# A list scheduler's model of transfers: issue time and one shared pipe, a margin at landing, and new places

## The chip, the cores and the metric

The kernel runs on one core of one Trainium2 chip. The metric is the device time of one launch in microseconds (us). The core has five instruction streams that run beside each other and wait for one another by semaphores: TensorE (PE in the profile, with its weight loads as PEld), VectorE (DVE), ScalarE (ACT), GpSimd (POOL) and SyncE (SP), which here issues all the transfers. Each engine works off its own stream strictly in the order in which the program was written.

## The reference

```
scores = q @ k.T / sqrt(64) - log(448)
attn   = sigmoid(scores);   x = attn @ v            # 8 batches, 12 heads, 448 x 64
x      = heads side by side                         # (8, 448, 768)
u      = x + (x.T @ U @ V).T                        # U 448 x 32, V 32 x 448
out    = u + relu(u @ w_ch1) @ w_ch2                # 768 -> 3072 -> 768
```

All inputs and the output are float32.

## The kernel before

Large float32 products are made of three float16 products: an operand is scaled by a power of two and split into a high part and a rest, and high x high, high x rest and rest x high are accumulated in one bank of PSUM. The eight banks, the weights (two buffers for each of w1 and w2), the loads of q, k and v (three and four buffers), and the results of attention (UA for batch 0, UB for the others) are all shared by what runs beside each other.

The work falls into these stages:

- Attention of batches 0 and 1 in float32 (the `whole` way, below `WHOLE` = 2): scores (L515), sigmoids on ACT (L631), products with v (L534, L544), then `mix` for U and V.
- The head: the feed-forward part (FFN) of batch 0 in six groups `g`, while the weights are decoded for the first time (`decode`, L836). They arrive as 64-bit words in 48 pieces of 768 KB: a load, three DVE instructions that make float32 of them (`to_f32`), a `bound` on ACT (L436, an absolute sum for the scale), a scale, the high part on ACT or POOL, the rest on DVE (L382). A decoded weight is written to `scratch` in DRAM for the later batches.
- The middle: the FFN of batches 1 to 3 (`ffn_in` L894, `ffn_out` L914) with weights fetched from `scratch`, and beside it the attention of batches 2, 4, 3, 5, 6 and 7 in the split way. There each pair of heads is prepared first: a `bound` of q, k and v, its maximum over the partitions by two transfers (`scale_by_dma`, L408), high parts on POOL, rests on DVE. `mix_half` transposes by a transfer (L803) ahead of its products (L811). `quarter_sums` and `far_forms` prepare sums of weights and of inputs for the last stage.
- The last stage (from about 985 us): the FFN of batches 4 to 7 in two pairs, as products of 2 x 2 blocks with seven instead of eight multiplications (L1089), on forms prepared in DRAM.

The order of all instructions is made by a planner (`Plan`). Every step is entered with `op`: engine, a cost, its operands, a place `pos`, a slack and a landing time. Places are not times, though they are written in the same unit: `order` (L127) simulates all engines, takes the engine and step that can start first, and among those of an engine that can start at that moment the step with the lowest place. What comes out is only the order on each engine and the buffers chosen, and `emit` writes the instructions in that order. A wrong cost therefore doesn't change what is computed; it changes which step stands ahead of which on an engine, where the one behind must wait.

The constants at L60 to L68 set the places. `START` and `ROOM0`, `ROOM` lay the FFN of the four plain batches out: `BEGIN[0]` = `START`, `BEGIN[1]` = `BEGIN[0]` + 163.6 + `ROOM0`, and so on. `BEFORE`, `PACE` and `MIXED1` place the attention of batch 1 and its mixing, `AHEAD`, `PREP` and `BOUNDS` those of the later ones. `DECODE` is how far ahead of a group's place its decode is placed, `EV_IN` and `EV_OUT` by how much the evictions of `ffn_in` and `ffn_out` are placed ahead of their products. `LEAD`, `SUMS`, `STEP_K` and `STEP_I` place the loads and sums of the last stage. A transfer was planned by `load` (L358) as

```
op("SP", max(0.6, n / 0.30e6), ..., land=2.0)
```

so SP is held until its `n` bytes have moved at 0.30 MB per us, and the data is there 2.0 us later. Other transfers had their own costs: the transpose 1.0 and 7.0, the copies to `forms` 0.6 and 3.0. In both versions SP may not start a transfer before the eighth last one has landed.

Of the kernel before, what the change touches and what calls it, by code (L numbers as in the profile page):

```python
# [37 lines left out]
P = 128  # L38
D = 64
# [50 lines left out]
class Plan:  # L90
# [36 lines left out]
    def order(self):  # L127
# [17 lines left out]
        done, port, landed, mode = [], 0.0, [0.0] * 8, 128  # L145
# [21 lines left out]
        while len(done) < n:  # L167
# [58 lines left out]
def fused_kernel(ctx: ExitStack, tc: tile.TileContext, q, k, v, wu, wv, w1, w2, out):  # L226
# [131 lines left out]
    def load(dst, src, n, reads, writes, pos, land=2.0):  # L358
        op("SP", max(0.6, n / 0.30e6), lambda: nc.sync.dma_start(out=dst(), in_=src()), reads, writes, pos, land=land)
# [14 lines left out]
    def pe(cost, fn, reads, writes, pos, slack=0.8, after=(), modes=(128, 128)):  # L374
        return op("PE", cost, fn, reads, writes, pos, slack, 0.3, after, modes=modes)
# [32 lines left out]
    def scale_by_dma(parts, kp, n, name, pos):  # L408
# [3 lines left out]
        load(lambda: far.x, lambda: parts.x[:, :n], 0.18e6, kp, [far], pos, 4.5)  # L412
        load(lambda: row.x[:, : n * P], lambda: far.x.rearrange("p n -> (p n)").partition_broadcast(P), 0.2e6, [far], [row], pos, 5.0)
        m, x = (lambda: e.x[:, :n]), (lambda: e.x[:, n : 2 * n])
        dve(0.15 + n * 0.13, lambda: nc.vector.tensor_reduce(
            out=m(), in_=row.x[:, : n * P].rearrange("q (p n) -> q n p", n=n), axis=AX.X, op=ALU.max), [row], [e], pos)
        dve(0.17, lambda: ts(nc.vector, x().bitcast(I32), m().bitcast(I32), 0x7F800000, ALU.bitwise_and), [e], [e], pos)
        pool(0.35, lambda: ts(nc.gpsimd, inv.x, x(), 2.0 ** -100, ALU.max, 1.0 / TOP, ALU.mult), [e], [inv], pos)
# [56 lines left out]
    def shifted(at):  # L475
        pool(0.5, lambda: nc.gpsimd.memset(ux, 0.0), (), ["ux", "vraw"], at)
        dve(0.25, lambda: nc.vector.tensor_copy(ux[0:64, 0], ua[0:64, 3]), [("ua", i) for i in range(4)] + ["ux"], ["ux"], at)
        load(lambda: ux[64:128, :, 3], lambda: ua[0:64, :, 0], 0.18e6, [("ua", 0), "ux"], ["ux"], at, 4.5)
        load(lambda: ux[0:64, 1:4, 3], lambda: ua[64:128, 0:3, 0], 0.18e6, [("ua", 0), "ux"], ["ux"], at, 4.5)
# [71 lines left out]
    def pair(b, p, at, d):  # L551
# [20 lines left out]
        else:  # L572
# [5 lines left out]
            for i in range(2):  # L578
                bound(lambda i=i: qk.x[:, i, :], S, lambda i=i: ss.x[:, i : i + 1], kqk[2 * i : 2 * i + 2], (ss, i), prep - BOUNDS, 0.73)
            bound(lambda: v32.x.rearrange("p a b -> p (a b)"), 512, lambda: ss.x[:, 2:3], [(v32, 0), (v32, 1)], (ss, 2), prep - BOUNDS, 0.82)  # L580
            s, inv = scale_by_dma(ss, [(ss, i) for i in range(3)], 3, "qkv", prep - BOUNDS + 1)
            cc, cv = sm("c", 1), sm("cv", 1)
            pool(0.5, lambda: ts(nc.gpsimd, cc.x, inv.x[:, 0:1], inv.x[:, 1:2], ALU.mult, 1.0 / math.sqrt(D), ALU.mult), [inv], [cc], prep + 1)
            pool(0.45, lambda: ts(nc.gpsimd, cv.x, inv.x[:, 2:3], 1.0 / A_UP, ALU.mult, 1.0, ALU.mult), [inv], [cv], prep + 1)
            pool(0.45, lambda: ts(nc.gpsimd, cm.x[mine], cc.x[mine], 1.0, ALU.mult, 1.0, ALU.mult), [cc], [(cm, odd)], prep + 1)
# [12 lines left out]
            for i in (1, 0):  # L598
# [3 lines left out]
                dve2(0.63, lambda i=i: rest(part(2 * i + 1), qk.x[:, i, :], s.x[:, i : i + 1], part(2 * i)),  # L602
                    ki + [s, (st, 2 * i)], [(st, 2 * i + 1)], prep + 3)
            pool(0.65, lambda: scaled(parts_v(0), v32.x[:, :3], s.x[:, 2:3]), [(v32, 0), s], [(sv, 0)], prep + 6, plan.wrote["decoded"])
            dve2(0.58, lambda: rest(parts_v(1), v32.x[:, :3], s.x[:, 2:3], parts_v(0)), [(v32, 0), s, (sv, 0)], [(sv, 1)], prep + 7)
            pool(0.45, lambda: scaled(last_v(0)[mine], v32.x[mine, 3], s.x[mine, 2:3]), [(v32, 1), s], [(v3, odd, 0)], prep + 7, plan.wrote["decoded"])
            dve2(0.25, lambda: rest(last_v(1)[mine], v32.x[mine, 3], s.x[mine, 2:3], last_v(0)[mine]), [(v32, 1), s, (v3, odd, 0)], [(v3, odd, 1)], prep + 8)
# [70 lines left out]
    def fetch_u(b, side, pos):  # L678

        u32s[b] = [plan.tile(f"u{side}{c}", [(UA if side == "a" else UB)[c]]) for c in range(NP)]  # L680
        for c in range(NP):
            load(lambda c=c: u32s[b][c].x, lambda c=c: parked[b][:, c], P * S * 4, [("parked", b, c)], [u32s[b][c]], pos + 3.0 * c, 2.5)
# [87 lines left out]
    def u_parts(b, at):  # L770
# [5 lines left out]
        for c in range(NP):  # L776
            hi, lo = (us, c, 0), (us, c, 1)
            if c % 2:
                pool(0.75, lambda c=c: scaled(us.x[:, c, 0, :], u32[c].x, su.x), [ku[c], su], [hi], at)
            else:  # L780
                act(0.65, lambda c=c: nc.scalar.activation(us.x[:, c, 0, :], u32[c].x, AF.Copy, scale=su.x), [ku[c], su], [hi], at)
            dve2(0.63, lambda c=c: rest(us.x[:, c, 1, :], u32[c].x, su.x, us.x[:, c, 0, :]), [ku[c], su, hi], [lo], at)
# [6 lines left out]
    def mix_half(b, hf, pos):  # L789
# [6 lines left out]
        for c in cs:  # L796
            i = c % 3
            if i == 1:
                pool(0.75, lambda c=c, i=i: scaled(xs.x[:, i, 0], u32[c].x, sx.x), [u32[c], sx], [(xs, i, 0)], pos)
            else:  # L800
                act(0.65, lambda c=c, i=i: nc.scalar.activation(xs.x[:, i, 0], u32[c].x, AF.Copy, scale=sx.x), [u32[c], sx], [(xs, i, 0)], pos)
            dve2(0.63, lambda c=c, i=i: rest(xs.x[:, i, 1], u32[c].x, sx.x, xs.x[:, i, 0]), [u32[c], sx, (xs, i, 0)], [(xs, i, 1)], pos)
        op("SP", 1.0, lambda: nc.sync.dma_start_transpose(out=xt.x, in_=xs.x.rearrange("p c x s -> p (c x s)")),  # L803
           [(xs, i, x) for i in range(3) for x in range(2)], [xt], pos + 1.0, land=7.0)
# [31 lines left out]
    def decode(i, g, pos):  # L836
# [5 lines left out]
        for n in range(NPIECE):  # L842
# [4 lines left out]
            bound(lambda t=t: t.x, PIECE, lambda n=n: ss.x[:, n : n + 1], [t], (ss, n), pos + n, 1.03, w64)  # L847
# [5 lines left out]
        for n, t in enumerate(made):  # L853
# [3 lines left out]
            if g == 0 and (i == 0 or n % 2):  # L857
                pool(1.5, lambda t=t, cut=cut: scaled(w.x[:, 0, cut], t.x, s.x), [t, s], [hi], at)
# [77 lines left out]
    def quarter_sums(i, g, f, pos, b=None, after=(), copy_after=()):  # L936
# [17 lines left out]
        for n_, r, c in ((A11, 0, 0), (A12, 0, 1), (A22, 1, 1)):  # L954
            for x in range(2):
                op("SP", 0.6, lambda n_=n_, r=r, c=c, x=x: nc.sync.dma_start(out=far(n_, x), in_=cut(far_w, r, c, x)),
                   [("scratch", i, g)], [("forms", i, n, n_, x)], pos, land=3.0, after=copy_after)
                done.append(("forms", i, n, n_, x))
        four_ = ((1, 0), (1, 1), (0, 0), (0, 1))
        if b is None:  # L960
            w = plan.tile("wsrc", WSRC)
            for j, (r, c) in enumerate(four_):
                for x in range(2):
                    op("SP", 0.7, lambda j=j, r=r, c=c, x=x: nc.sync.dma_start(out=w.x[:, x, j], in_=cut(far_w, r, c, x)),
                       [("scratch", i, g)], [(w, j, x)], pos - 8, land=2.5, after=after)
# [6 lines left out]
        for j in range(4):  # L972
            pool(1.0, lambda j=j: nc.gpsimd.tensor_tensor(out=t.x[:, j], in0=quarter(j, 0), in1=quarter(j, 1), op=ALU.add),  # L973
# [7 lines left out]
        dve2(1.9, lambda: nc.vector.tensor_tensor(out=o.x[:, :, :, 1], in0=t.x.rearrange(order), in1=o.x[:, :, :, 0], op=ALU.subtract),  # L981
             [(t, j) for j in range(4)] + [(o, 0)], [(o, 1)], pos)
        load(lambda: far(slice(S3, S4 + 1), slice(0, 2)), lambda: o.x, P * 24 * P * 2, [(o, 0), (o, 1)], [("forms", i, n, S3)], pos + 1, 3.0)
# [25 lines left out]
    def far_forms(b0, b1, su, pos, step):  # L1009
# [7 lines left out]
        def get(c, r, n):  # L1017
            t, b, part = place(), (b0, b1)[n], c + 3 * r
            op("SP", 0.8, lambda: nc.sync.dma_start(out=t.x, in_=parked[b][:, part]), [("parked", b, part)], [t], at[0], land=2.5)
# [330 lines left out]
```

## Time and profile before

| | us |
|---|---|
| median of 3 runs | 1586.39 (1579.51 to 1586.65) |
| the profiled execution | 1570.29 |
| its span, first to last instruction | 1568.5 |
| ACT busy in it | 815.4 |
| POOL busy in it | 398.7 |

A profile is one execution. Busy time of an engine is the union of its instructions; PE's instructions are pipelined. In the views below, a row of a timeline has the start, the duration, the engine, the line and the operation, output <- inputs, shapes and count, and in brackets the idle time of the engine before it with what ended it. Releasers are inferred from semaphores: the last one to come is named, not what held it up in its turn.

### The profile page before, as it was taken

The page shows a single profiled execution, that of the slowest core. Times are in us where ns is not written, and L with a number is a line of the kernel's source. Part 1 is how long each engine was busy: PE and PEld are TensorE (multiplying, and loading weights), DVE is VectorE, ACT ScalarE, POOL GpSimd, SP SyncE. Part 2 cuts the span into 40 slices and gives each one's busy share as a digit, 9 for nine tenths or more (in the row PEclk, how much of TensorE's full clock was granted, in tenths as well). Part 3 has the DMA queues.
Part 4 walks back from the last instruction along what each step waited for, and adds up shares of the span by engine and source line. Part 5 has one row for each costly group of instructions (what it writes and reads, how often), then busy time and mean ns, then how long its engine had stood idle before and what let it go on. Part 6 is the DMA issues. An engine that isn't in the chain of part 4 may idle for free.

```text
span 1568.5 us, 24119 instructions
## 1 busy us (share of the span) xinstructions
PE 1529.3 (98%) x8843; PEld 753.5 (48%) x8843; DVE 1134.4 (72%) x1904; ACT 815.4 (52%) x1455; POOL 398.7 (25%) x537
## 2 busy tenths in 40 slices
PE   8989989999999999999999999999999999999999
PEld 3345444444444444444444444555555555555554
DVE  2889989777677777777787846776767878564656
ACT  6667655278657567766877653332423614121310
POOL 0100002553323553223212362064454400000000
PEclk9999999999999999999999999999999999999999
DMA  6878887877776877756778547886656673333331
GB/s 216 275 274 291 286 275 245 286 263 187 152 226 153 241 248 201 203 169 172 212 226 232 137 153 246 288 266 196 199 176 195 253 265 123 106 111 136 106 106 71
DMA packets 212567, 320.19 MB, mean 204 GB/s; under 512 B 130016, under 2 KB 178528, under 8 KB 200160
## 3 DMA queue, kind: packets, MB, share of 16 engines
q1 hardware_dynamic: 212448, 318.65, 65.5%
q8 instruction: 69, 1.13, 0.3%
q14 instruction: 50, 0.41, 0.1%
HBM read 247.04 MB, written 77.42 MB: 207 GB/s over the span
## 4 chain that ended last, share of the span: by engine, by line
PE 84%; DVE 7%; DMA 5%; ACT 2%; issue 1%; SPq 0%; POOL 0%; ACTq 0%; DVEq 0%; POOLq 0%
PE bank L1089 36%; PE bank L894 18%; PE bank L914 15%; PE bank L534 5%; PE bank L515 5%; DVE stg L382 1%; DMA qk__99<-k_in 1%; PE bank L544 1%; PE bank L519 1%; DVE a L382 1%; DMA qk__100<-k_in 1%; PE bank L811 1%; ACT at L631 1%; DMA w<-w_in 1%; DVE w__89 L382 0%
## 5 line engine op out<-in xcount | busy, mean ns | idle before, releaser
L382 DVE SCALAR_TENSOR_TENSOR a<-at,a 128x896 f16<-128x896 f32 x126 | 142.0, 1146 | 32.0 <-ACT a L661 31.5
L914 PE MATMUL bank<-h__92,w__90 128*128 128x448 f16 x792 | 158.3, 353 | 0.0
L914 PE MATMUL bank<-h__93,w__91 128*128 128x448 f16 x792 | 157.9, 353 | 0.0
L894 PE MATMUL bank<-us__86,w__88 128*128 128x448 f16 x648 | 130.8, 359 | 7.4 <-DVE ua__74 L382 4.4
L894 PE MATMUL bank<-us__86,w__89 128*128 128x448 f16 x648 | 129.8, 356 | 3.9 <-DVE ua__74 L382 2.7
L894 PEld LDWEIGHTS <-w__88 128*128 128x128 f16 x864 | 84.8, 99 | 92.1 <-issue 17.1
L894 PEld LDWEIGHTS <-w__89 128*128 128x128 f16 x864 | 83.5, 98 | 87.7 <-issue 13.1
L914 PEld LDWEIGHTS <-w__90 128*128 128x128 f16 x864 | 82.4, 98 | 83.1 <-issue 9.8
L914 PEld LDWEIGHTS <-w__91 128*128 128x128 f16 x864 | 82.7, 98 | 82.4 <-issue 9.0
L661 ACT ACTIVATE a<-at 128x896 f16<-128x896 f32 x126 | 116.1, 959 | 0.8
L1089 PEld LDWEIGHTS <-w__89 128*128 128x128 f16 x819 | 80.1, 98 | 74.8 <-issue 0.4
L1089 PEld LDWEIGHTS <-w__88 128*128 128x128 f16 x756 | 74.0, 98 | 69.0
L1089 PEld LDWEIGHTS <-w__91 128*128 128x128 f16 x756 | 74.0, 98 | 68.9
L977 POOL TENSOR_TENSOR w<-w 128x384 f32<-128x384 f32 x96 | 104.4, 1087 | 4.7
L1089 PEld LDWEIGHTS <-w__90 128*128 128x128 f16 x693 | 67.8, 98 | 64.1 <-issue 0.9
L515 PE MATMUL bank<-stg 64*128 64x448 f16 x648 | 75.1, 351 | 3.0 <-ACT at L631 1.9
L973 POOL TENSOR_TENSOR w<-w 128x384 f32<-128x384 f16 x48 | 45.9, 980 | 125.6 <-DVE xnt L981 82.2
L534 PE MATMUL bank<-a,stg 128*64 128x448 f16 x648 | 69.6, 360 | 0.4 <-DVE a L382 0.4
L379 POOL TENSOR_SCALAR inv_qkv__211<-e_qkv__208 128x3 f32<-128x3 f32 x12 | 3.8, 314 | 210.8 <-DVE e_qkv__208 L379 210.7
L631 ACT ACTIVATE at<-bank,bias_s,c__219 128x448 f32<-128x448 f32 x72 | 47.6, 722 | 12.0 <-PE bank L515 5.6
L980 ACT CAST xnt<-w 128x1536 f16<-128x1536 f32 x24 | 35.3, 1471 | 34.6 <-POOL w L977 33.1
L901 ACT ACTIVATE r__94<-bank 128x448 f32<-128x448 f32 x48 | 25.9, 539 | 50.1 <-PE bank L894 50.0
(1132 smaller groups left out, 3150.6 us busy)
## 6 DMA issues: line engine op xcount, KB each, us to landing
w<-w_in SPq DMA_DIRECT2D x48, 768.0 KB, 5.6
forms<-xnt SPq DMA_DIRECT2D x24, 768.0 KB, 4.6
w__89<-forms SPq DMA_DIRECT2D x13, 1344.0 KB, 5.9
w__88<-forms SPq DMA_DIRECT2D x12, 1344.0 KB, 5.7
w__91<-forms SPq DMA_DIRECT2D x12, 1344.0 KB, 5.9
w__90<-forms SPq DMA_DIRECT2D x11, 1344.0 KB, 5.8
forms<-scratch SPq DMA_DIRECT2D x144, 96.0 KB, 3.9
w__88<-scratch SPq DMA_DIRECT2D x9, 1536.0 KB, 8.2
```

The source lines that it names most:

```text
L382: nc.vector.scalar_tensor_tensor(out=out, in0=in0, scalar=s, in1=in1, op0=op0, op1=op1)
L515: nc.tensor.matmul(sc[j, h].x[:, :S], x[rows_of(h), j * P : j * P + P], y[rows_of(h)], start=i == 0, stop=i == n - 1)
L534: nc.tensor.matmul(av.x[rows_of(h), :S], x[:, j, rows_of(h)], y(tiles[j], h), start=j == 0 and i == 0, stop=not quad and j == 2 and i == n ...
L631: act(cost, lambda: nc.scalar.activation(out_(), in_(), AF.Sigmoid, bias=bias_s, scale=c if whole else by.x), kin + ["bias"] + ([] if whol ...
L661: act(0.95, lambda a=a, to=to: nc.scalar.activation(half(a, 0), to.x, AF.Copy, scale=A_UP), kto, [(a, 0)], here + A_OFF)
L894: nc.tensor.matmul(ph.x[:, :S], wx[:, x, c, f * P : (f + 1) * P], us.x[:, c, y, :], start=c == 0 and i == 0, stop=c == NP - 1 and i == 2,)
L901: act(0.54, lambda: nc.scalar.activation(r.x, ph.x[:, :S], AF.Relu, scale=DOWN_H), [ph], [r], pos - EV_IN)
L914: nc.tensor.matmul(po.x[:, :S], wx[:, x, f, e * P : (e + 1) * P], h.x[:, f, y, :], start=f == 0 and i == 0, stop=f == FC - 1 and i == 2,)
L973: pool(1.0, lambda j=j: nc.gpsimd.tensor_tensor(out=t.x[:, j], in0=quarter(j, 0), in1=quarter(j, 1), op=ALU.add), [(w, j, 0), (w, j, 1)] i ...
L977: pool(1.0, lambda o_=o_, x=x, y=y, sub=sub: nc.gpsimd.tensor_tensor(out=t.x[:, o_], in0=t.x[:, x], in1=t.x[:, y], op=ALU.subtract if sub ...
L980: act(1.45, lambda: nc.scalar.copy(o.x[:, :, :, 0], t.x.rearrange(order)), [(t, j) for j in range(4)], [(o, 0)], pos)
L1089: nc.tensor.matmul(bank.x[:, :S], wt.x[:, k, FACTOR[n], x], both(f)[:, y], start=start and k == i == 0, stop=k == 2 and i == 2, skip_group ...
```

## The change

Three things in the planner, and nothing in the instructions.

A transfer holds SP only for its issue (0.42 to 0.7 us, 3.9 for the transpose). Its bytes then go through one pipe at 0.33 MB per us, shared by all transfers, and the data is there 3.7 us after they are through (some have 0.3 to 1.5 more). The end so told also frees the buffers. Some costs of ACT, DVE and POOL steps are corrected by some hundredths to 0.5 us. `LATE` keeps the slack of PE's steps at the 0.8 that it had. All places are set anew.

```diff
-ROOM0, ROOM, AHEAD, BEFORE, PACE = 43.592, 38.551, 48.926, 33.326, 1.302
-PREP, BOUNDS, VALUES, SECOND, MIXED = 13.847, 6.504, 1.154, 1.456, 5.983
+PIPE, LANDS, LATE = 0.33e6, 3.7, 0.8
+
+ROOM0, ROOM, AHEAD, BEFORE, PACE = 48.642, 37.714, 43.993, 32.439, 0.773
+PREP, BOUNDS, VALUES, SECOND, MIXED = 14.614, 6.948, 0.934, 1.54, 5.841
...
-MIXED1, MIX_1 = 5.122, 11.442
-MIX_2, EV_IN, EV_OUT, A_OFF = 15.998, 27.927, 4.965, 2.867
-START, DECODE = 46.447, 54.64
-U_AT, U_STEP = 3.978, 5.376
-LEAD, SUMS, STEP_K, STEP_I, FFN_LEAD = 25.837, 10.607, 53.168, 15.955, 3.531
+MIXED1, MIX_1 = 6.343, 11.488
+MIX_2, EV_IN, EV_OUT, A_OFF = 15.418, 39.745, 5.316, 2.39
+START, DECODE = 51.103, 36.212
+U_AT, U_STEP = 4.07, 4.76
+LEAD, SUMS, STEP_K, STEP_I, FFN_LEAD = 13.515, 7.66, 39.428, 15.982, 5.745
...
+            told = end[i] + o[6]
             if e == "SP":
-                landed.append(end[i] + o[6])
+                pipe = max(pipe, end[i]) + o[9][0] / PIPE
+                told = pipe + o[6]
+                landed.append(told)
...
-                x.got.free = max(x.got.free, end[i] + o[6])
+                x.got.free = max(x.got.free, told)
...
-                at = end[i] + (o[6] + x[5] if x[0] != e or e == "SP" else 0.0 if e == "PE" else 0.14)
+                at = told + x[5] if x[0] != e or e == "SP" else end[i] + (0.0 if e == "PE" else 0.14)
...
-    def load(dst, src, n, reads, writes, pos, land=2.0):
-        op("SP", max(0.6, n / 0.30e6), lambda: nc.sync.dma_start(out=dst(), in_=src()), reads, writes, pos, land=land)
+    def load(dst, src, n, reads, writes, pos, more=0.0, cost=0.42):
+        dma(cost, n, lambda: nc.sync.dma_start(out=dst(), in_=src()), reads, writes, pos, more)
+
+    def dma(cost, n, fn, reads, writes, pos, more=0.0, after=()):
+        op("SP", cost, fn, reads, writes, pos, land=LANDS + more, after=after, modes=(n, 0))
...
-                     D * S * 4, [], [(qk, i, h)], early)
+                     D * S * 4, [], [(qk, i, h)], early, cost=0.62)
...
-            for i in range(2):
-                bound(lambda i=i: qk.x[:, i, :], S, lambda i=i: ss.x[:, i : i + 1], kqk[2 * i : 2 * i + 2], (ss, i), prep - BOUNDS, 0.73)
+            for i in range(2):
+                bound(lambda i=i: qk.x[:, i, :], S, lambda i=i: ss.x[:, i : i + 1], kqk[2 * i : 2 * i + 2], (ss, i), prep - BOUNDS, 0.68)
...
-        op("SP", 1.0, lambda: nc.sync.dma_start_transpose(out=xt.x, in_=xs.x.rearrange("p c x s -> p (c x s)")),
-           [(xs, i, x) for i in range(3) for x in range(2)], [xt], pos + 1.0, land=7.0)
+        dma(3.9, 0.2e6, lambda: nc.sync.dma_start_transpose(out=xt.x, in_=xs.x.rearrange("p c x s -> p (c x s)")),
+           [(xs, i, x) for i in range(3) for x in range(2)], [xt], pos + 1.0, 0.3)
...
-                pool(1.5, lambda t=t, cut=cut: scaled(w.x[:, 0, cut], t.x, s.x), [t, s], [hi], at)
+                pool(1.0, lambda t=t, cut=cut: scaled(w.x[:, 0, cut], t.x, s.x), [t, s], [hi], at)
```

More of the change, by code (lines that the diff above doesn't have):

```diff
@@ L144, in order @@
                 cand[o[0]].append(i)
-        done, port, landed, mode = [], 0.0, [0.0] * 8, 128
+        done, port, landed, mode, pipe = [], 0.0, [0.0] * 8, 128, 0.0
         def room(i):
@@ L955, in quarter_sums @@
             for x in range(2):
-                op("SP", 0.6, lambda n_=n_, r=r, c=c, x=x: nc.sync.dma_start(out=far(n_, x), in_=cut(far_w, r, c, x)),
-                   [("scratch", i, g)], [("forms", i, n, n_, x)], pos, land=3.0, after=copy_after)
+                dma(0.62, 98304, lambda n_=n_, r=r, c=c, x=x: nc.sync.dma_start(out=far(n_, x), in_=cut(far_w, r, c, x)),
+                   [("scratch", i, g)], [("forms", i, n, n_, x)], pos, after=copy_after)
                 done.append(("forms", i, n, n_, x))
@@ L972, in quarter_sums @@
         for j in range(4):
-            pool(1.0, lambda j=j: nc.gpsimd.tensor_tensor(out=t.x[:, j], in0=quarter(j, 0), in1=quarter(j, 1), op=ALU.add),
+            pool(0.93, lambda j=j: nc.gpsimd.tensor_tensor(out=t.x[:, j], in0=quarter(j, 0), in1=quarter(j, 1), op=ALU.add),
                  [(w, j, 0), (w, j, 1)] if b is None else kw_of(w), [(t, j)], pos)
@@ L1064, in u_forms @@
                 b, part, t = (b0, b1)[n], c + 3 * r, spot("u")
-                op("SP", 0.8, lambda t=t, b=b, part=part: nc.sync.dma_start(out=t.x, in_=parked[b][:, part]),
-                   [("parked", b, part)], [t], at - 3, land=2.5, after=after)
+                dma(0.44, P * S * 4, lambda t=t, b=b, part=part: nc.sync.dma_start(out=t.x, in_=parked[b][:, part]),
+                   [("parked", b, part)], [t], at - 3, after=after)
                 act(0.6, lambda t=t: nc.scalar.activation(t.x, t.x, AF.Copy, scale=su.x), [t, su], [t], at)
```

58 lines of the change are left out of this document (29 added, 29 removed).

## The prediction

> **What bounds the kernel now.** I read the page first, then the busy time by stage, then PE's waits and the instructions around each. The page, its head, part 1 and the first line of part 4:
>
> ```profile
> span 1568.5 us, 24119 instructions
> PE 1529.3 (98%) x8843; PEld 753.5 (48%) x8843; DVE 1134.4 (72%) x1904; ACT 815.4 (52%) x1455; POOL 398.7 (25%) x537
> ...
> PE 84%; DVE 7%; DMA 5%; ACT 2%; issue 1%; SPq 0%; POOL 0%; ACTq 0%; DVEq 0%; POOLq 0%
> ```
>
> PE is busy for 1529.3 of 1568.5 us. The change leaves the instructions as they are and moves them, so all it can win lies in the other 39.2 us, and in matmuls that run at a reduced clock. By stage (start and end, length, busy time of PE, PEld, DVE, ACT, POOL, then granted clock, DMA share, GB/s):
>
> ```profile
> 0.00:60.00 60.00, 54.78 (x265) 22.07 (x266) 27.10 (x45) 39.24 (x77) 5.41 (x12) 1.00 0.74 243
> 60.00:292.00 232.00, 212.86 (x1076) 103.10 (x1075) 214.81 (x399) 133.59 (x254) 24.30 (x36) 0.96 0.82 276
> 292.00:985.00 693.00, 682.50 (x4443) 328.73 (x4443) 499.06 (x837) 470.20 (x837) 250.73 (x375) 1.00 0.72 204
> 985.00:1568.50 583.50, 579.20 (x3063) 299.58 (x3061) 393.41 (x625) 172.32 (x289) 118.22 (x115) 1.00 0.51 172
> ```
>
> PE's idle time is 5.2 us in the first stretch (mostly the first loads), 19.1 in the head where the weights are decoded, 10.5 in the middle (batches 1 to 3 beside the attention of 2 to 7), and 4.3 in the last stretch, which contains the final write-out. In the head DVE is busy for 214.8 of 232 us, 93%: there it is nearly the bound, and the clock drops too. So there are two places to look at, the middle and the head.
>
> The middle first. Seven waits of PE there make up most of its 10.5 us. These rows show six of them, in order of time, each with what ACT did just ahead of it (in brackets: idle time before, and what ended it):
>
> ```profile
> 399.21 1.31 PE L515 MATMUL bank<-stg 64*128 64x448 f16 x12
> 402.62 0.58 ACT L436 ACTIVATE junk<-qk__99 128x448 bf16<-128x448 f32 x1 [3.86 <-DMA qk__99<-k_in]
> 404.74 2.58 ACT L631 ACTIVATE at<-bank,bias_s,c__217 128x448 f32<-128x448 f32 x4
> 405.52 0.65 PE L811 MATMUL bank<-w,ua 128*128 128x384 f16 x3 [2.63 <-ACT at L631]
> ...
> 435.65 0.66 PE L811 MATMUL bank<-w,ua 128*128 128x384 f16 x3 [0.93 <-DMA w<-w]
> ...
> 454.84 0.58 ACT L436 ACTIVATE junk<-qk__98 128x448 bf16<-128x448 f32 x1 [1.16 <-DMA qk__98<-k_in]
> 456.08 0.72 PE L515 MATMUL bank<-stg 64*128 64x448 f16 x5 [1.12 <-ACT ub__80 L671]
> ...
> 548.12 0.49 ACT L814 ACTIVATE xnt<-bank 128x384 f16<-128x384 f32 x1 [1.88 <-DMA forms<-xnt]
> 549.25 0.74 PE L820 MATMUL bank<-vst,xnt 128*128 128x448 f16 x3 [1.05 <-DVE xnt L382]
> ...
> 660.98 0.58 ACT L436 ACTIVATE junk<-qk__100 128x448 bf16<-128x448 f32 x1 [4.64 <-DMA qk__100<-k_in]
> 662.31 0.65 PE L811 MATMUL bank<-w,ua 128*128 128x384 f16 x3 [2.44 <-ACT at L631]
> ...
> 794.02 0.67 ACT L1020 ACTIVATE w<-w,s_u__239 128x448 f32<-128x448 f32 x1 [3.91 <-DMA w<-parked]
> 795.36 0.72 PE L515 MATMUL bank<-stg 64*128 64x448 f16 x5 [1.23 <-ACT at L631]
> ```
>
> The view names ACT or DVE as PE's releaser, but behind them stands a transfer. At 402.62 the head of ACT's queue is a bound (L436) that waited 3.86 us for a load; the sigmoids behind it, whose scores were done at 399.21 + 1.31 = 400.5, began at 404.74, and PE stood 2.63 us for a bank. The same happens at 456, 549, 662 and 795, and at 435 PE itself waits for the transpose. These six are 2.63 + 0.93 + 1.12 + 1.05 + 2.44 + 1.23 = 9.4 us. An engine works in the order the planner wrote down, and the planner thought that the data would be there.
>
> **The change: the model of a transfer.** What the trace has for transfers (KB each and median us from issue to landing; then SP's issues, with their own duration):
>
> ```profile
> w<-w_in SPq DMA_DIRECT2D x48, 768.0 KB, 5.6
> ...
> w__88<-forms SPq DMA_DIRECT2D x12, 1344.0 KB, 5.7
> ...
> w__88<-scratch SPq DMA_DIRECT2D x9, 1536.0 KB, 8.2
> ...
> qk__98<-k_in SPq DMA_DIRECT2D x36, 112.0 KB, 5.1
> ...
> qk__100<-q_in SPq DMA_DIRECT2D x30, 112.0 KB, 3.5
> ```
>
> ```profile
> 398.21 0.59 SPq L359 DMA_DIRECT2D qk__99<-k_in  x1
> ...
> 434.94 0.38 SPq L359 DMA_DIRECT2D w__90<-scratch  x1
> ...
> 649.50 3.93 SPq L803 DMA_TRANSPOSE w<-w  x1
> ```
>
> Old against new, from the code: a q or k load (114,688 bytes) was 0.6 + 2.0 = 2.6 us, and becomes 0.62 + 0.35 + 3.7 = 4.7; the trace has 3.5 to 5.1. A piece of weights was 2.6 + 2.0 = 4.6, and becomes 0.42 + 2.4 + 3.7 = 6.5; the trace has 5.6. A fetched weight was 5.2 + 2.0 = 7.2, and becomes 0.42 + 4.8 + 3.7 = 8.9; the trace has 8.2. It held SP for 5.2 us and now for 0.42; the trace has 0.38. The transpose held SP for 1.0 and now for 3.9; the trace has 3.93. So loads come 2.1 us later in the new plan, and whatever is queued on SP behind a transpose 2.9 later. Both are the size and the sign of ACT's waits (1.2 to 4.6 us), and the planner takes on each engine what can start first, so with honest landings the sigmoids of 400.5 stand ahead of the bound of 402.6.
>
> The DMA page of the Trainium skill ("DMA: Bandwidth & Descriptors", section "Anatomy of one DMA — SWDGE (gpsimd) path") speaks against this margin: a fixed 2.0 us plus bytes at 436 GB/s. By it a q or k load would take an estimated 2.3 us, the old plan was right, the middle would win nothing, and the time would be about 1579 instead of 1572. The trace disagrees, with 3.5 to 5.1 us here on SP's queue.
>
> **Middle, the term.** Bounds: a gain of 9.4 us plus a reduced clock at most; at worst a loss, since a plan in a new order has new places where reality runs late, and the nearest price for that is what the old one lost, so 5 us the other way (half of 10.5). The clock after the wait at 662 is in this slice:
>
> ```profile
> 640.00:680.00 40.00, 37.56 (x247) 17.79 (x246) 29.94 (x60) 25.63 (x49) 10.17 (x24) 0.96 0.71 204
> ```
>
> 4% of 40 us is 1.6. I take two thirds of 9.4 + 1.6, a gain of **7 us**: the landings vary from 3.5 to 5.1, so some waits return.
>
> **Head, the term.** Here the places do more than the transfers. PE's largest wait and the work on DVE ahead of it, a chain of the same length at full clock (118.27), and the last decode:
>
> ```profile
> 118.27 6.97 PE L894 MATMUL bank<-us__86,w__89 128*128 128x448 f16 x36
> 217.14 9.74 PE L894 MATMUL bank<-us__86,w__88 128*128 128x448 f16 x36 [4.40 <-DVE ua__74 L382]
> ```
>
> ```profile
> 213.33 0.95 DVE L382 SCALAR_TENSOR_TENSOR stg<-w,stg 128x768 int32<-128x768 int32 x1
> 214.20 0.55 DVE L379 TENSOR_SCALAR stg<-w 128x768 int32<-128x768 int32 x1
> 214.67 1.82 DVE L382 SCALAR_TENSOR_TENSOR stg<-w,stg 128x768 int32<-128x768 int32 x2
> 216.41 0.68 DVE L382 SCALAR_TENSOR_TENSOR ua__74<-bank,kg__169,ua__74 128x448 f32<-128x448 f32 x1
> ...
> 276.81 2.87 DVE L382 SCALAR_TENSOR_TENSOR w__91<-stg,s_w__186,w__91 128x768 f16<-128x768 f32 x3
> ```
>
> PE waited 4.40 us for a bank whose eviction (ua at 216.41) stood behind four decode instructions, and its next 36 matmuls then took 9.74 us instead of 6.97, 2.8 more. The new places speak to this. DECODE falls from 54.6 to 36.2, so decode yields 18.4 us more of place to evictions, and EV_IN rises from 27.9 to 39.7, so ffn_in's evictions gain 11.8. Attention 1's step falls from 1.302 x 207.2 / 7.6 = 35.5 to 0.773 x 212.2 / 7.6 = 21.6, and its mixing from place 13.1 + 5.122 x 35.5 = 195 to 18.7 + 6.343 x 21.6 = 155, so UB comes free sooner for attention 2, which can then fill PE's gaps. The other side: DVE's total work stays, and decode that yields is late for the FFN. Bounds: 19.1 us of waits and 0.04 x 232 = 9.3 us of clock, 28 in all, can go at most; a loss can reach the 18.4 us of place that decode gives up. I take a quarter of 28, a gain of **7 us**, since DVE at 93% leaves no more room than its 17.2 idle us, of which PE's waits see a part.
>
> **The rest, at nothing.** Calling a transfer's end by the pipe instead of the issue, and the corrected costs of bounds, POOL and DVE steps (0.03 to 0.5 us each), change the order alone; they lie in the two terms above. In the last stretch PE's idle time is 4.3 us with the final write-out, and LEAD, SUMS and STEP_K move loads and sums that PE's matmuls cover; a weight in forms is now planned at 0.42 + 4.2 + 3.7 = 8.3 us where the trace has 5.7, too careful, which orders it early. Without that cover, LEAD (25.8 to 13.5) would put forms 12.3 us later. Bounds: 0 to 8 us lost (two thirds of 12.3). I take 0, as PE has hardly a wait there. The start (first loads, 5.2 us) keeps its order, give or take 1 us.
>
> **The sum.** 7 + 7 = 14 us off the profiled execution's own 1570.29 us (span 1568.5 and 1.8 around it) is 1556. The median of the runs, 1586.39, stands 16.1 above that execution, and no row explains why; I let the difference stand and take 14 off it: **1572 us**.
>
> **The rivals.** (1) The head opens up: with UB free at place 155, attention 2 fills most of its gaps. It would take 18 of 28 us there and 9 in the middle, 27: 1559. For it speaks that PE's filler is all that is missing; against it, DVE at 93%.
> (2) The waits move. The static order meets landings from 3.5 to 5.1 us in other places, the middle wins 4 and the head nothing: 1582. For it: transfers ended only 5% of the chain of waits. The rule of the page, or a margin simply too wide, ends here too (1579).
> (3) Slower: decode comes late. Evictions go ahead of it, the last decode (276.81) moves later, and attention 1, already used up at a step of 21.6, can't fill. Price: the 18.4 us of place, and clock loss at 2.8 per 4.40 us for the third of it that comes as long waits (4), less the middle's 7: 15 more, 1601. It decides once that last decode starts about 15 us later than now, at 292, as then both gains are gone.
>
> **How the numbers follow.** A measurement here can tell about 0.5%, 8 us, from no change: faster is below 1578.5, slower above 1594.3. Chances: the forecast, 1564 to 1578, 0.40; rival 1, 1552 to 1564, 0.12; rival 2, 1578.5 to 1594, 0.30; rival 3, above, 0.18. That is 0.52 faster, 0.30 same, 0.18 slower. For 8 in 10 I leave out half of rival 1 and two thirds of rival 3: 1557 to 1597. The forecast's own range is 1564 to 1578.
>
> **What would show it.** Right: in the middle PE's idle time falls from 10.5 to about 4 us, and ACT's waits for q and k loads no longer stand ahead of PE's waits for sigmoids; behind a transpose SP's order has other things than loads that are due. In the head PE's idle time falls from 19.1 to about 14 and the clock rises from 0.96; evictions no longer wait behind decode; the last decode starts before 285. Wrong: middle waits of the same sum on other transfers (rival 2), or PE waiting for decoded weights before 292 (rival 3), or a gap where the last stretch turns to its second pair of batches.

## The result and the profile after

The changed kernel takes **1567.39 us** (1563.51 to 1570.98, 4 runs) against 1585.97 us for the kernel before beside it: a ratio of 0.989, interval 0.986 to 0.993. The forecast was 1572. But its three terms did not come in as forecast: the middle won about as much as was said or more (6.5 and 12.4 us against 7), the head lost where it was to win, and the last stage lost where it was to stay.

The page of the changed kernel, its head, part 1 and the first line of part 4:

```profile
span 1569.2 us, 24164 instructions
...
PE 1529.2 (97%) x8843; PEld 750.8 (48%) x8843; DVE 1131.6 (72%) x1904; ACT 812.1 (52%) x1455; POOL 390.5 (25%) x537
...
PE 83%; DVE 8%; DMA 5%; ACT 2%; POOL 1%; issue 1%; SPq 0%; POOLq 0%; ACTq 0%; DVEq 0%
```

By stage, in the columns of the prediction (start and end, length, busy time of PE, PEld, DVE, ACT, POOL, granted clock, DMA share, GB/s):

```profile
0.00:60.00 60.00, 54.71 (x255) 21.46 (x257) 29.80 (x57) 39.21 (x76) 4.74 (x12) 1.00 0.79 247
60.00:292.00 232.00, 209.31 (x1068) 99.28 (x1065) 208.28 (x380) 133.52 (x255) 20.66 (x29) 0.96 0.86 279
292.00:985.00 693.00, 688.96 (x4496) 332.95 (x4494) 503.52 (x849) 469.93 (x838) 246.22 (x381) 1.00 0.72 204
985.00:1569.20 584.20, 576.22 (x3030) 297.13 (x3028) 389.95 (x620) 169.48 (x287) 118.91 (x115) 0.99 0.51 170
```

These two profiled executions do not show the gain: 1570.98 us here, 1570.29 before. The one of before lies below every run of its series (1579.51 to 1586.65), the one of after at the top of its own. So both kernels were run again as they are, in one series (labels e1_before and e2_after), and there the profiled executions are ordinary ones: 1573.99 where the median was 1575.75, and 1565.33 where it was 1565.48. The page and the stages of the kernel before, run again:

```profile
PE 1529.3 (97%) x8843; PEld 753.8 (48%) x8843; DVE 1135.0 (72%) x1904; ACT 816.4 (52%) x1455; POOL 399.6 (25%) x537
...
60.00:292.00 232.00, 212.77 (x1083) 103.30 (x1081) 216.06 (x401) 133.80 (x254) 25.41 (x38) 0.96 0.82 277
292.00:985.00 693.00, 679.31 (x4402) 326.85 (x4401) 498.96 (x835) 470.07 (x835) 250.00 (x374) 1.00 0.71 202
985.00:1572.20 587.20, 582.82 (x3099) 301.19 (x3096) 393.02 (x625) 173.11 (x290) 118.74 (x115) 1.00 0.51 173
```

and of the changed kernel, run again:

```profile
PE 1525.7 (98%) x8843; PEld 749.7 (48%) x8843; DVE 1130.0 (72%) x1904; ACT 812.2 (52%) x1455; POOL 387.9 (25%) x537
...
60.00:292.00 232.00, 208.79 (x1076) 99.49 (x1073) 209.23 (x381) 133.75 (x256) 19.84 (x29) 0.97 0.87 281
292.00:985.00 693.00, 691.71 (x4511) 334.55 (x4509) 505.71 (x856) 471.12 (x840) 245.83 (x382) 1.00 0.71 205
985.00:1563.50 578.50, 570.55 (x3007) 294.44 (x3004) 384.67 (x612) 168.02 (x284) 117.49 (x114) 1.00 0.51 170
```

PE's idle time in a stage is the stage's length less PE's busy time. In this pair it goes from 19.2 to 23.2 us in the head (+4.0), from 13.7 to 1.3 in the middle (-12.4), and from 4.4 to 8.0 in the last stage (+3.6); the start is the same to 0.2. That is 5.1 us less in sum, and PE is busy for 3.6 us less with the same 8843 matmuls: 8.7 us, the whole difference of the spans (1572.2 less 1563.5). The medians differ by 10.3 us.

**The middle** shows what the change is for. In the timeline of the changed kernel, run again (start, duration, engine, line and operation; in brackets the idle time before and its releaser), ACT still waits for a k load, longer than any wait of ACT in the prediction's rows, and PE's rows on both sides go on without a wait:

```profile
446.17 2.43 PE L921 MATMUL bank<-h__93,w__91 128*128 128x448 f16 x12
...
447.91 0.58 ACT L443 ACTIVATE junk<-qk__99 128x448 bf16<-128x448 f32 x1 [6.50 <-DMA qk__99<-k_in]
448.44 1.87 PE L901 MATMUL bank<-us__87,w__88 128*128 128x448 f16 x9
```

Transfers have not become faster: a k load takes 5.1 us (median) from issue to landing in the kernel before and 5.3 in the changed one. What PE needs of ACT now stands ahead of the instruction that waits, not behind it. The kernel before still has its late loads; at the place that the prediction showed at 794, its timeline when run again and the 40 us around it (the columns of the stages):

```profile
794.76 0.67 ACT L1020 ACTIVATE w<-w,s_u__239 128x448 f32<-128x448 f32 x1 [5.73 <-DMA w<-parked]
796.09 1.27 PE L515 MATMUL bank<-stg 64*128 64x448 f16 x5 [3.06 <-ACT at L631]
```

```profile
780.00:820.00 40.00, 36.94 (x235) 16.68 (x233) 28.02 (x55) 29.23 (x50) 6.74 (x14) 0.91 0.70 229
```

and the same 40 us of the changed kernel, run again:

```profile
780.00:820.00 40.00, 40.00 (x272) 19.17 (x271) 31.95 (x62) 37.14 (x69) 13.73 (x23) 1.00 0.72 231
```

In the execution that the prediction was made from, this transfer kept ACT for 3.91 us and PE for 1.23; here 5.73 and 3.06, and the clock stands at 0.91 over the 40 us (in every 2 us from 796 to 802 it is 0.50). The size of these waits differs between executions of one and the same order; the changed order has 40.00 of 40 us busy.

**The head** has the pattern that was to go. Its largest wait in the changed kernel, and the last decode, in the timeline:

```profile
224.42 0.61 DVE L447 TENSOR_REDUCE mx__155<-ub__85 128x1 f32<-128x448 f32 x1
224.95 0.55 DVE L386 TENSOR_SCALAR stg<-w 128x768 int32<-128x768 int32 x1
...
225.95 3.56 DVE L389 SCALAR_TENSOR_TENSOR stg<-w,stg 128x768 int32<-128x768 int32 x4
229.42 0.55 DVE L386 TENSOR_SCALAR stg<-w 128x768 int32<-128x768 int32 x1
229.89 0.68 DVE L389 SCALAR_TENSOR_TENSOR ua__74<-bank,kg__169,ua__74 128x448 f32<-128x448 f32 x1
230.62 0.90 PE L921 MATMUL bank<-h__93,w__91 128*128 128x448 f16 x2 [8.95 <-DVE ua__74 L389]
...
293.04 1.93 DVE L389 SCALAR_TENSOR_TENSOR w__91<-at,s_w__186,w__91 128x768 f16<-128x768 f32 x2
```

An eviction again stands behind decode instructions, and PE waits 8.95 us, from 221.7 on, where before the worst wait was 4.40. About 5 us of it are decode (224.95 to 229.89); in the 3.3 us before, DVE makes evictions and sums of batch 1's mixing (`ub`, `mx`). DVE is busy for 208.3 us of the stage instead of 214.8, and the last decode begins at 293 (291.6 when run again) instead of 277: decode did yield, and became late.

**The last stage** has new waits of 1.36, 2.26 and 0.72 us, 4.3 together, all at one place. POOL, DVE and PE there in the timeline (POOL's rows left out are 16 steps with no idle time noted before them):

```profile
1221.96 1.14 POOL L1078 TENSOR_TENSOR a<-stg,us__87 128x448 f32<-128x448 f32 x1 [26.43 <-DVE h__93 L389]
...
1236.06 0.68 DVE L389 SCALAR_TENSOR_TENSOR stg<-bank,fg,qk__99 128x448 f32<-128x448 f32 x1 [1.01 <-PE bank L1096]
1236.66 0.61 DVE L389 SCALAR_TENSOR_TENSOR stg<-v__101,stg 128x448 f16<-128x448 f32 x1
1237.19 1.46 DVE L1149 TENSOR_TENSOR a<-stg,a 128x448 f16<-128x448 f32 x1
1238.57 1.55 DVE L389 SCALAR_TENSOR_TENSOR a<-a 128x448 f16<-128x448 f32 x1
1238.70 0.54 PE L1096 MATMUL bank<-a,w__90 128*128 128x448 f16 x2 [1.36 <-DVE a L1149]
1240.04 1.55 DVE L1083 TENSOR_TENSOR us__86<-at,us__86 128x448 f16<-128x448 f32 x1
1243.16 1.03 POOL L1083 TENSOR_TENSOR qk__99<-qk__100,qk__99 128x448 f16<-128x448 f32 x1 [0.68 <-ACT qk__99 L1081]
1244.22 0.63 DVE L1125 TENSOR_TENSOR qk__100<-v__102,stg 128x448 f32<-128x448 f32 x1 [2.63 <-POOL qk__99 L1083]
1246.03 0.35 PE L1096 MATMUL bank<-v__102,w__90 128*128 128x448 f16 x1 [2.26 <-ACT v__102 L1133]
1247.10 0.90 PE L1096 MATMUL bank<-v__102,w__90 128*128 128x448 f16 x2 [0.72 <-DVE v__102 L1134]
```

From 1222 to 1244 POOL makes the sums and rests of the second pair's forms (L1078, L1083) almost without a break. Beside them three of the DVE steps shown take 1.46 to 1.55 us instead of 0.61, while those that read a bank of PSUM, as the one at 1236.06, keep their 0.68. A later step waits 2.63 us for POOL. Of PE's 4.3 us, 1.36 stand behind a lengthened step and the other 2.98 behind the one that waited. In the kernel before, POOL has a pause of 12.24 us at this place, between 1238.8 and the row below; PE's one wait in that stage is 0.6 us.

```profile
1251.07 1.14 POOL L1071 TENSOR_TENSOR h__93<-stg,a 128x448 f32<-128x448 f32 x1 [12.24 <-ACT stg L1067]
```

### The profile page after: what moved, and what is told of

Same layout as the page of the kernel before. It is cut to its first block, busy times and chain, and to the rows that moved or that the text cites. A ratio compares the mean times of both kernels' runs of the same rounds, so it can differ in the third digit from the quotient of the medians.

```text
span 1569.2 us, 24164 instructions
## 1 busy us (share of the span) xinstructions
PE 1529.2 (97%) x8843; PEld 750.8 (48%) x8843; DVE 1131.6 (72%) x1904; ACT 812.1 (52%) x1455; POOL 390.5 (25%) x537
## 4 chain that ended last, share of the span: by engine, by line
PE 83%; DVE 8%; DMA 5%; ACT 2%; POOL 1%; issue 1%; SPq 0%; POOLq 0%; ACTq 0%; DVEq 0%
PE bank L1096 36%; PE bank L921 17%; PE bank L901 17%; PE bank L522 5%; PE bank L541 5%; DMA row__116<-far 1%; DMA w<-w_in 1%; DVE us__87 L389 1%; DVE stg L389 1%; PE bank L551 1%; DMA qk__98<-q_in 1%; PE bank L526 1%; PE bank L818 1%; DMA v__101<-v_in 1%; DVE at L389 0%
## 5 line engine op out<-in xcount | busy, mean ns | idle before, releaser
L921 PE MATMUL bank<-h__93,w__91 128*128 128x448 f16 x792 | 160.7, 357 | 9.9 <-DVE ua__74 L389 8.9
L921 PE MATMUL bank<-h__92,w__90 128*128 128x448 f16 x792 | 158.6, 353 | 3.0 <-ACT h__93 L909 1.3
L389 DVE SCALAR_TENSOR_TENSOR a<-at,a 128x896 f16<-128x896 f32 (+1 forms) x129 | 142.2, 1125 | 18.9 <-ACT a L668 18.6
L921 PEld LDWEIGHTS <-w__90 128*128 128x128 f16 x864 | 81.8, 98 | 88.3 <-issue 13.7
L901 PE MATMUL bank<-us__86,w__88 128*128 128x448 f16 x432 | 84.5, 353 | 1.8 <-DVE e_u__161 L408 1.5
L901 PE MATMUL bank<-us__86,w__89 128*128 128x448 f16 x432 | 85.5, 354 | 0.0
L901 PE MATMUL bank<-us__87,w__89 128*128 128x448 f16 x432 | 85.4, 353 | 0.0
L901 PE MATMUL bank<-us__87,w__88 128*128 128x448 f16 x432 | 85.1, 353 | 0.0
```

The costliest lines, as they stand in the source:

```text
L389: nc.vector.scalar_tensor_tensor(out=out, in0=in0, scalar=s, in1=in1, op0=op0, op1=op1)
L901: nc.tensor.matmul(ph.x[:, :S], wx[:, x, c, f * P : (f + 1) * P], us.x[:, c, y, :], start=c == 0 and i == 0, stop=c == NP - 1 and i == 2,)
L921: nc.tensor.matmul(po.x[:, :S], wx[:, x, f, e * P : (e + 1) * P], h.x[:, f, y, :], start=f == 0 and i == 0, stop=f == FC - 1 and i == 2,)
```

## The experiments

All twelve runs in one table. "Idle" is PE's idle time, a stage's length less PE's busy time. The kernel before gave a median of 1575.4 us beside e1 to e4, 1584.9 beside e5 to e8 and 1585.1 beside e9 to e12, so kernels of different groups are compared by their ratios and not by their times. The changed kernel's own ratio was 0.989 in one group and 0.993 in another: a difference of 0.004 between groups says nothing. An idle time is that of one execution; where a kernel has two, they differ by up to 0.5 us in the head and 3.2 in the middle.

| run | us | ratio to before (interval) | idle head | idle middle | idle last |
|---|---|---|---|---|---|
| e1 before again | 1575.75 | 1.000 (0.998 to 1.002) | 19.2 | 13.7 | 4.4 |
| e2 changed kernel again | 1565.48 | 0.993 (0.991 to 0.996) | 23.2 | 1.3 | 8.0 |
| e3 model alone | 1581.92 | 1.004 (1.003 to 1.005) | 31.6 | 3.2 | 8.4 |
| e4 places alone | 1590.93 | 1.010 (1.008 to 1.013) | 29.3 | 12.2 | 9.3 |
| e5 landing 2.0 | 1619.85 | 1.021 (1.018 to 1.024) | 38.3 | 19.3 | 9.3 |
| e6 SP held by bytes | 1571.35 | 0.991 (0.988 to 0.993) | 22.3 | 0.0 | 8.3 |
| e7 `DECODE` back | 1575.35 | 0.993 (0.991 to 0.995) | 28.6 | 0.0 | 10.1 |
| e8 attention 1 back | 1589.47 | 1.002 (1.000 to 1.003) | 37.9 | 1.7 | 9.3 |
| e9 `DECODE` + 1 | 1580.24 | 0.997 (0.995 to 0.999) | 31.1 | 4.2 | 9.2 |
| e10 late forms | 1563.30 | 0.987 (0.985 to 0.989) | 23.6 | 3.3 | 3.7 |
| e11 SP held, late forms | 1565.17 | 0.988 (0.986 to 0.990) | 22.5 | 0.0 | 3.7 |
| e12 landing 3.0 | 1573.19 | 0.993 (0.991 to 0.996) | 20.1 | 4.6 | 7.8 |

**Model and places apart (e1 to e4).** e1 and e2 are the two kernels unchanged; what they gave stands above.

> The kernel before, unchanged, for another profile of it. Its profiled execution took 1570.3 us where the others took 1579.5 to 1586.7. Theory A (transfers that land late): an ordinary execution is at about 1583, its ratio to the kernel before is 1.000 within 0.002, and what it has more than the first profile is PE's idle time in the middle (292 to 985 us), 18 to 25 us instead of 10.5, behind transfers. Rival B (the clock): its PE idle time is about 39 us as before, and the time is in a lower granted clock. Rival C: nothing of the two, and PE's busy time itself is longer.

> The changed kernel, unchanged, for a second profile and a tighter interval: ratio 0.989 within 0.003. Theory A: PE's idle time in the middle is 3 to 7 us again, as its first profile has 4.0, that is it varies less from execution to execution than that of the kernel before. Rival B and C: the middle is the same and the clock or PE's busy time is what differs from e1.

Both missed. The kernel before was at 1575.75 and not 1583, with 13.7 us idle in the middle and not 18 to 25; the changed kernel's ratio was 0.993, just above the range, with 1.3 us in the middle, below it.

e3 has the new model and costs with the old values at L60 to L68; e4 the old `load`, costs and `order` with the new values.

```diff
# e3, in the changed kernel (all the places so)
-START, DECODE = 51.103, 36.212
+START, DECODE = 46.447, 54.64
# e4, in the kernel before (all the places so)
-START, DECODE = 46.447, 54.64
+START, DECODE = 51.103, 36.212
```

> The new model of transfers and the corrected costs with the old places. Theory A (honest landings make the gain, the places little): ratio 0.985 to 0.995, PE idle in the middle 3 to 8 us, in the head (60 to 292) 17 to 25. Rival D (the places make it): ratio 0.997 to 1.010, middle idle at 10 us or more.

> The new places with the old model and the old costs. Theory A: middle idle of 10 us or more again, behind loads of q and k that ACT's bounds wait for; ratio 1.00 to 1.01. Rival D: ratio 0.985 to 0.995, middle idle at 3 to 8 us.

The head and the middle of e3:

```profile
60.00:292.00 232.00, 200.37 (x999) 92.87 (x996) 205.58 (x372) 131.34 (x248) 23.68 (x29) 0.93 0.86 277
292.00:985.00 693.00, 689.78 (x4495) 332.60 (x4494) 503.07 (x856) 473.27 (x845) 250.47 (x382) 1.00 0.70 202
```

and of e4:

```profile
60.00:292.00 232.00, 202.73 (x1002) 95.45 (x999) 204.64 (x381) 126.83 (x246) 15.14 (x26) 0.92 0.80 265
292.00:985.00 693.00, 680.78 (x4391) 328.59 (x4390) 492.35 (x834) 463.22 (x830) 247.41 (x384) 1.00 0.69 201
```

Each part alone makes the kernel slower, by 0.4 and 1.0%; both together make it faster. For e4 theory A holds; for e3 it holds in the middle alone, as the time and the head (31.6 us) lie outside what it said. The middle goes with the model, whatever the places: 10.5 to 13.7 us idle under the old one (before, e1, e4), 1.3 to 4.0 under the new (e3, after, e2). The head goes with neither alone: 19 us with both old, 23 with both new, 29 to 32 with one of each. The new places take back 8.4 of the 12.4 us that the new model costs there (31.6 to 23.2 against 19.2 to 31.6); under the model for which they were not set they cost 10.

**Which part of the model (e5, e6, e12).** e5 and e12 plan landings of 2.0 and 3.0 us instead of 3.7. e6 keeps 3.7 but holds SP until the bytes have moved, as before, with no pipe; the transpose keeps its new 3.9.

```diff
# e5 (e12: 3.0)
-PIPE, LANDS, LATE = 0.33e6, 3.7, 0.8
+PIPE, LANDS, LATE = 0.33e6, 2.0, 0.8
# e6
-                pipe = max(pipe, end[i]) + o[9][0] / PIPE
-                told = pipe + o[6]
...
-        op("SP", cost, fn, reads, writes, pos, land=LANDS + more, after=after, modes=(n, 0))
+        op("SP", max(cost, n / 0.30e6), fn, reads, writes, pos, land=LANDS + more, after=after, modes=(n, 0))
```

> The changed kernel with the landing back at 2.0 us after the pipe (LANDS 3.7 to 2.0); issue times, pipe, costs and places as changed. Theory A1 (the margin at landing is what the middle needed): PE idle in the middle rises from the 1.3 to 4.0 us of the changed kernel to 8 us or more, ratio 1.000 to 1.010. Rival A2 (issue times and the pipe are what it needed): the middle stays under 6 us. The head may go either way by 10 us, as its places were set for 3.7.

> The changed kernel with SP held for a transfer's bytes as before (at 0.30 MB per us) and no shared pipe; the landing of 3.7 us, the transpose's 3.9, costs and places as changed. Theory A1: the middle stays under 6 us. Rival A2: the middle rises to 8 us or more, behind fetched weights and what is planned after them. The head may go either way by 10 us.

> The changed kernel with a landing of 3.0 us, between 2.0 (19.3 us of PE idle in the middle) and 3.7 (1.3 to 4.0). Theory A1a (a mean landing is enough, the margin above it isn't needed): the middle stays under 6 us. Theory A1b (the margin above the mean is what keeps the varying transfers away from PE): 7 to 15 us. The head may go either way by 10 us.

The middle of e5, and one of its waits in the timeline:

```profile
292.00:985.00 693.00, 673.75 (x4313) 324.83 (x4312) 485.60 (x823) 451.47 (x814) 249.87 (x383) 0.99 0.67 193
```

```profile
546.51 0.58 ACT L443 ACTIVATE junk<-qk__100 128x448 bf16<-128x448 f32 x1 [6.71 <-DMA qk__100<-k_in]
...
548.71 1.27 PE L522 MATMUL bank<-stg 64*128 64x448 f16 x5 [4.39 <-ACT at L638]
```

the middle of e6:

```profile
292.00:985.00 693.00, 693.00 (x4517) 334.78 (x4516) 518.30 (x866) 475.39 (x846) 251.57 (x384) 1.00 0.71 208
```

and of e12:

```profile
292.00:985.00 693.00, 688.36 (x4474) 331.38 (x4473) 511.71 (x853) 468.85 (x838) 256.05 (x382) 1.00 0.73 204
```

With a planned landing of 2.0 the old pattern is back: a bound at the head of ACT's queue for 6.71 us, sigmoids behind it, and PE without a bank for 4.39, the longest wait of the stage. With 3.0 the middle is idle for 4.6 us, as with 3.7 in one of its executions (4.0). So the size of the landing makes the middle. That any disturbed order would do the same is not so: with changed places, e7 to e9 below, the middle stays at 0.0 to 4.2 us. A mean landing does nearly what the margin does: that the margin is needed is not shown. Issue time and pipe, two of the three parts of the new transfer, are not needed: e6 without them has no idle time in the middle at all, and its ratio, 0.991, can't be told from the two of the changed kernel (0.989 and 0.993). So theories A1 and A1a hold; e5's head (38.3) and time (2.1%) went further up than was said. Whether the transpose's 3.9 us on SP matter was not tried alone.

The Trainium skill ("DMA: Bandwidth & Descriptors", section "Anatomy of one DMA — SWDGE (gpsimd) path") gives the fixed part as about 2.0 us plus bytes. It gives this for transfers issued from GpSimd, and those here are issued from SyncE, so no run here tests the figure itself. A plan with that fixed part on SyncE's queue is e5, with 2.1% more time than the kernel before; though e5's places were set for 3.7.

**The head's places (e7 to e9).** e7 puts `DECODE` back, e8 the places of attention 1. e9 moves `DECODE` by 1.0, a step that means nothing, to see how much any change of place does here.

```diff
# e7 (e9: 37.212)
-START, DECODE = 51.103, 36.212
+START, DECODE = 51.103, 54.64
# e8
-ROOM0, ROOM, AHEAD, BEFORE, PACE = 48.642, 37.714, 43.993, 32.439, 0.773
+ROOM0, ROOM, AHEAD, BEFORE, PACE = 48.642, 37.714, 43.993, 33.326, 1.302
-MIXED1, MIX_1 = 6.343, 11.488
+MIXED1, MIX_1 = 5.122, 11.488
```

> The changed kernel with DECODE back at 54.64, all else as changed. Theory E (as predicted, the lower DECODE lets evictions go ahead and helps the head): PE idle in the head, 22.7 and 23.2 us in the two profiles of the changed kernel, rises to 27 or more. Rival F (the lower DECODE starves the head): it falls to 19 or less. Rival G (one place alone hardly matters, what matters is the set): it stays within 3 us. The middle stays under 6 us by all three.

> The changed kernel with the places of attention 1 back (BEFORE, PACE and MIXED1 of the kernel before: step 36.4 instead of 21.6), all else as changed. Theory E (an early attention 1 leaves PE without filler later in the head, and costs): PE idle in the head falls from about 23 to 19 us or less. Rival H (it frees UB sooner and helps): it rises to 27 or more. The middle stays under 6 us by both.

> A control: the changed kernel with DECODE at 37.212 instead of 36.212, a change of place that means nothing. Theory I (the head's outcome hangs on the exact set of places, and single places say little): PE idle in the head moves by 4 us or more from the 22.7 and 23.2 of the changed kernel, in either direction, so that the 28.6 with DECODE back isn't told from it. Theory J (the head answers to places smoothly): it stays within 2 us. The middle stays under 6 us by both, if the landing model is what makes it.

The head of e7, where the 18.4 us of `DECODE` are undone:

```profile
60.00:292.00 232.00, 203.38 (x1027) 96.00 (x1026) 205.65 (x376) 131.82 (x251) 20.09 (x29) 0.93 0.85 276
```

and of e9, where it is 1.0:

```profile
60.00:292.00 232.00, 200.90 (x1016) 93.79 (x1013) 202.71 (x363) 127.77 (x245) 16.28 (x26) 0.96 0.86 277
```

The nudge costs the head 7.9 us (31.1 against 23.2), more than the whole of `DECODE` (28.6). Attention 1's places cost most, 14.7 (37.9), and 6.8 of that stand above the nudge. So e7, which by itself would speak for theory E, says nothing of `DECODE`, and theory I holds. e8 went the way of rival H and against E, and part of it may be attention 1's own. No other place was tried alone. The head hangs on the exact set of numbers.

**The last stage (e10, e11).** If POOL's unbroken run is what delays DVE and PE there, loading the last third of the second pair's inputs later must break the run and end the waits. All these loads wait for the start of an earlier product, `begun[-8]`; now those of c = 2 wait for one that starts five products later:

```diff
                 dma(0.44, P * S * 4, lambda t=t, b=b, part=part: nc.sync.dma_start(out=t.x, in_=parked[b][:, part]),
-                   [("parked", b, part)], [t], at - 3, after=after)
+                   [("parked", b, part)], [t], at - 3, after=after if c < 2 else [begun[-3]])
```

e10 is the changed kernel with this edit, e11 is e6 with it.

> The changed kernel, with the loads of the third group of input forms for the second pair of batches held back until the third last product of the first pair (before: the eighth last, for all three groups). Theory K (POOL's unbroken run of 18 subtractions in the changed kernel, beside which DVE's steps take 1.5 instead of 0.6 us, makes PE's waits of 4.4 us in the last stage): those waits fall to 1 us or less and the ratio to the kernel before is 0.002 to 0.003 lower than the changed kernel's. Rival L (they come from the transfers): they stay, or come back as a wait for the forms.

> The same edit on the version with SP held and no pipe (landing 3.7), which had no PE wait in the middle, 22.3 us in the head and 4.7 in the last stage. Theory K: the last stage's waits fall to 1 us or less, the middle stays at 0 to 2, the ratio to the kernel before is 0.986 to 0.989, below that of both kernels. Rival L: 0.990 as without the edit.

The same place in e10's timeline:

```profile
1234.51 1.03 POOL L1083 TENSOR_TENSOR qk__98<-v__103,qk__98 128x448 f16<-128x448 f32 x1
...
1235.94 0.61 DVE L1149 TENSOR_TENSOR stg<-v__104,stg 128x448 f16<-128x448 f32 x1
...
1239.49 1.87 POOL L1078 TENSOR_TENSOR stg<-a,us__87 128x448 f32<-128x448 f32 x1 [3.95 <-ACT a L1074]
```

and e10's last stage:

```profile
985.00:1561.60 576.60, 572.95 (x3031) 296.42 (x3029) 387.31 (x620) 170.12 (x287) 118.92 (x115) 1.00 0.52 173
```

POOL pauses for 3.95 us, the DVE step at L1149 takes 0.61 us again instead of 1.46, and the stage's idle time falls from 8.0 and 8.3 to 3.65 us in both kernels, below the 4.3 of before, with no wait of PE noted in it. So theory K holds: POOL's run makes these waits. How much of them is the longer steps and how much the wait for POOL is not separated, as the pause ends both.

Not every idle time of that column has this cause. In e4, e5, e8 and e9 (9.2 to 9.3 us) the stage has instead one wait of PE of 5.5 to 5.7 us for a load of prepared forms, here e4's in the view of waits:

```profile
PE bank L1089 <- DMA w__88<-forms: 5.6, 1, 5.6
```

e10 is the fastest kernel of this study, 1.3% below before. It was not timed in one series with the changed kernel, and its interval (0.985 to 0.989) meets that of the changed kernel's first series (0.986 to 0.993); that it is faster rests on the stage row.

The Trainium skill ("SBUF — State Buffer", section "🔬 SBUF: two separate sides") tells of a port pair of DVE and GpSimd that is an exclusive lock for a whole instruction. The trace agrees in kind: beside POOL's steps the lengthened DVE steps are as long as their own 0.61 us and most of one POOL step more (1.46 to 1.55).

## Why the prediction was right, and where it was not

**Middle, 7 us: right in mechanism, too small in size.** The waits went from behind the transfers as forecast, and the 4 us forecast to be left are 4.04 in the profile after. Against the profile that the forecast was made from that is a gain of 6.5. In the ordinary pair it is 12.4, above the stated bound of 9.4 and a reduced clock, since an ordinary execution of before has 13.7 us there to win and not 10.5. Waits of ACT for q and k loads still occur (6.50 us at 448); as the prediction said, what changed is who stands behind them: no wait of PE in the middle of either profile of the changed kernel names a sigmoid. SP's hold by a fetched weight (5.2 us planned, 0.38 in the trace), set beside the landing in that part, is not needed for the gain: e6 still holds SP so.

**Head, 7 us: wrong in sign.** It lost 3.6 to 4.0, and the clock stayed at 0.96 to 0.97. The step that failed is "I take a quarter of 28, a gain of 7 us": it added up what each place would let the evictions do, as if places were times. e3 shows that the model itself disturbs the head by 12.4 us, which the sum had at nothing ("change the order alone"), and e9 that a move of 1.0 costs 7.9. Evictions do still stand behind decode (about 5 us of the wait of 8.95). Which of the places would make the head better stays open.

**Last stage, 0: wrong by 3.6, within its bounds of 0 to 8, and not by the step named.** `LEAD` is not the cause: e3 has the old `LEAD` and 8.4 us idle, with the same three waits (1.36, 2.68 and 0.66). It was POOL's run beside DVE, which the part "at nothing" did not look at. The sign that the prediction gave, a gap where the stage turns to its second pair of batches, came true.

**Start, 0: right.** 0.2 us in the ordinary pair.

**The sum and the offset.** Of 14 us forecast, 8.7 are in the spans of the ordinary pair and 10.3 in the medians of that series; in the first series the medians stand 18.6 apart. Letting the 16.1 us between profile and median stand gave 1572, near to 1567.4, but partly by luck: the loss of 7.6 in head and last stage was paid by a larger middle (5.4 above the term) and by 3.6 us less of busy PE. That last item fits the clock, as the row from 780 to 820 goes from 0.91 to 1.00 (0.09 x 40 = 3.6), though other slices differ too. Why the kernel before takes 1575 us in one series and 1585 in three others, where the changed one differs by 2 us between its two, stays open: there is no profile of an execution of before at 1585. The series at 1575 ran on another chip than the later two at 1585 (for the first the record names none), and its executions of before have a mean granted clock of 0.991 against 0.988; by that ratio an estimated 4 of the 10 us would be the clock.

**The rivals.** Rival 1 fell: the head did not open up. Rival 2, waits that move, is not what happened in the middle. Its other way, that a landing of 2.0 was right and the middle wins nothing, fell too: e5 plans with 2.0 and has 19.3 us idle there. The prediction set a figure for transfers issued from GpSimd against a queue of SyncE, so the fault was in the use of the figure. A margin simply too wide, its last part, is not borne out in the middle; e12's head (20.1 with 3.0 against 23.2) hints at it, in a stage where a nudge does more than that. Rival 3's mechanism happened: the last decode begins at 293.0 and 291.6 in the two profiles, at its mark of 292, and DVE is less busy. Its price did not: 4 us of idle time and not 18, and the middle's gain remained.

## What to carry to other kernels

A static order is as good as its planned landing times where one instruction that waits at the head of a queue keeps others from an engine that bounds the kernel: plan a mean landing from the trace, 3.0 to 3.7 us here and not 2.0, before modelling anything finer. Places tuned under one cost model belong to it: here each of the two, changed alone, made the kernel slower. So change model and places together; and a nudge of one place by a step that means nothing should be run before any place is given a reason. Take the profile of an ordinary execution, one near its median, before working out terms from its waits.

## What the runs showed of the hardware

Two executions of one program in one order differ by more in a wait than the change was to win there: 3.91 and 5.73 us of ACT for the same transfer, 1.23 and 3.06 of PE behind it. After the 3.06 us the granted clock was 0.50 from 796 to 802 us. And a series of POOL steps is not free for a DVE step beside it: 0.61 us became 1.46 to 1.55 in three steps, in the length of the instruction, where no wait is noted. DVE steps that read a bank of PSUM kept their 0.68 us beside the same run.
